# A second set of seven products in the first dense layer of a fused attention and MLP kernel

## The chip, the cores and the metric

The kernel runs on one core of one Trainium2 chip. The metric is the device time of one execution in microseconds (us); several executions are made and their median is given. Engines are called TensorE (PE, with PEld for its weight loads), VectorE (DVE), ScalarE (ACT), GpSimd (POOL) and SyncE (SP, which here issues DMAs). PSUM is the memory that TensorE writes; it has eight banks, and a tile of 128 x 512 f32 fills one.

## The reference: what is computed

Linear attention with decay over 4 batches, 8 heads, 768 positions and head size 64, then a two-layer MLP on the 3072 x 512 result:

```python
for b in range(nb):                                   # blocks of positions
    intra = einsum(qb, kb) * Dmask ; intra = intra @ vb
    inter = (qb * lam_pow) @ kv_state
    out[:, :, sl] = intra + inter
    kv_state = lam_block * kv_state + (kb * rev_pow).T @ vb
x = out as (3072, 512)
h = x @ w_in                                          # 512 -> 2048
g = h * tanh(softplus(h))                             # Mish
return g @ w_out                                      # 2048 -> 512
```

## The kernel before

**Groups.** The 768 positions are cut into six groups of 128 (`n` = 0 to 5). A group takes the same 128 positions of all four batches, so it has 512 tokens. For each group the kernel computes attention into `xt[n]` (512 features on 4 x 128 partitions, 512 tokens), the first layer and Mish into `hsg[n]` (16 units `ni` of 128 hidden features), and the second layer into the output. Attention of group n+1 is worked in between the matmuls of group n. There is no scheduler: the Python order of the calls is the order in every engine's queue. The loop from line 776 writes this order out: `units` is a list of short pieces of TensorE work, and after unit `u` come the extras that `visit`, `turns`, `sums`, `slots` and the last lines of the loop (L845) name for that number. "uN" below is unit N of that list.

**First layer.** `mm1_duo(n, g, lo, hi)` (L422) does units 2g and 2g+1 for half of the tokens: 8 matmuls of 128 x 256 into one `ph` bank, then one Mish on ScalarE (L441). In groups 2 to 5 (called `d` = 2 in the code) duos 0 to 5 cover units 0 to 11. Units 12 to 15 go through `set_unit` (L506): a Strassen-like product of 2 x 2 quarters (two input halves, two pairs of units, two token halves) with seven products P1 to P7 of 4 matmuls each, where a plain product takes 8 times 4. It needs sums of weight quarters (`isum`, made once in group 0), sums of quarters of `xt` (`xsum`, four VectorE operations, recorded at L496, after u6), and sums between products. Sums run through PSUM: P1's result is copied to SBUF (`u1`) and P2 added on top in the same bank; step "open" copies `u1` into another bank `z`, and P6 is added there; P6's sum is copied to a bank `y`, and P7 and P3 are added to `z` and `y`; P5's result is copied to SBUF (`p5`, ScalarE) and VectorE adds it to `z` and `y` (`hs`, L543) ahead of Mish; at the end P4 is added to `z`.

**Second layer.** `fast_unit` (L663) does the whole second layer by the same scheme in 14 units (seven products, two 128-token blocks each, 8 matmuls per unit). Its sums of `hsg` are `gsum` (`token_sum`, L574, VectorE).

**Attention in between.** `pair_a` (8 matmuls `pv`, then VectorE sums and the next state), `pair_s` (16 score matmuls `pS` and 16 state matmuls into the two `pO` banks, then four masked copies `sb` on VectorE) and `pair_o` (16 matmuls into the `pO` banks; four scalings `xtok` on VectorE at L384, and for each batch a transposing DMA from SP into `xt[n+1]`). Each handles two batches, and a group calls them for batches 0, 1 (s) and 2, 3 (t); t of group n fills the second token half of `xt[n+1]`. `turn` scales a k chunk (VectorE, `ktil`) and issues two transposing DMAs on SP (`qraw`, `kraw`).

**PSUM banks.** Tags and banks: `ph` 2, `po` 2, `pS`, `pk`, `pO`, `pq` one each. A matmul into a bank waits until the last reader of the bank's former tile is done.

**Loads.** k, q and v chunks are loaded by GpSimd's queue into `kn`, `qn` (8 buffers each) and `vz`, paced by one-element copies (`pace`) that wait for a Mish.

Of the kernel before, what the change touches and what calls it, by code (L numbers as in the profile page):

```python
# [7 lines left out]
F32 = mybir.dt.float32  # L8
# [12 lines left out]
def kernel(  # L21
# [125 lines left out]
    lbm = const.tile([128, JP, 128], F32, name="lbm")  # L147
# [22 lines left out]
    lq = const.tile([128, JP, C], F32, name="lq")  # L170
# [197 lines left out]
    def pair_o(s):  # L368

        n = s.n  # L370
        if xt[n] is None:
            xt[n] = work.tile([128, JP, GT], F16, name="xt", tag="xt", bufs=2)
        for t in range(2):
            for m, b in enumerate(s.bs):
                for j in range(JP):
                    nc.tensor.matmul(  # L376
                        s.pO[t][:, m, j, :], s.sb[m][t][:, j, :],
                        vz[(n * B + b) % NVB][:, 2 * j + t, 0:D],
                        start=False, stop=True, skip_group_check=True)
        xtok = [work.tile([128, JP, 2, D], F16, name="xtok", tag="xtok", bufs=4) for _ in s.bs]  # L380
        lt = lqt.rearrange("p (j t) -> p j t", t=2)
        for m, b in enumerate(s.bs):
            for t in range(2):
                nc.vector.tensor_tensor(out=xtok[m][:, :, t, :], in0=s.pO[t][:, m],  # L384
                                        in1=bc(lt[:, :, t], 2, D), op=ALU.mult)
            nc.sync.dma_start_transpose(
                out=xt[n][:, :, b * C : (b + 1) * C],
                in_=xtok[m].rearrange("p j t e -> p (j t e)"))
# [32 lines left out]

    def mm1_duo(n, g, lo, hi):  # L422

        if hsg[n] is None:
            hsg[n] = work.tile([128, NKI, GT], F16, name="hsg", tag="hsg", bufs=2)
        h = GT // 2
        half = lo // h
        if (n, g, half) not in duo_t:
            duo_t[n, g, half] = ps.tile([128, 2, h], F32, name="ph", tag="ph", bufs=2)
        t = duo_t[n, g, half]  # L430
        for m in range(2):
            ni = 2 * g + m
            for kc in range(NKC):
                nc.tensor.matmul(  # L434
                    t[:, m, lo - half * h : hi - half * h],
                    w_in(ni, kc),
                    xt[n][:, kc, lo:hi], start=(m == 0 and kc == 0), stop=(kc == NKC - 1),
                    skip_group_check=True,
                )
        if hi == half * h + h:  # L440
            nc.scalar.activation(hsg[n][:, 2 * g : 2 * g + 2, half * h : half * h + h], t, AF.Mish)  # L441
            mark.append(hsg[n][0:1, 2 * g, half * h : half * h + 1])
# [21 lines left out]
    SU = NKI - 4  # L464
    isum = [const.tile([128, KH, 256], F16, name=f"isum{i}") for i in range(4)]

    def i_quarter(r, c):

        t = win[-1]
        return t[:, r * KH : (r + 1) * KH, c * 256 : (c + 1) * 256]  # L470

    def in_sum(i):

        a, b, op = (
            lambda: (i_quarter(0, 1), i_quarter(0, 0), ALU.subtract),
            lambda: (i_quarter(1, 1), isum[0], ALU.subtract),
            lambda: (i_quarter(1, 1), i_quarter(0, 1), ALU.subtract),
            lambda: (i_quarter(1, 0), isum[1], ALU.subtract),
        )[i]()
        nc.vector.tensor_tensor(out=isum[i], in0=a, in1=b, op=op)  # L480
# [17 lines left out]
    first = {}  # L498

    def mish(n, r, c, src):  # L500

        nc.scalar.activation(
            hsg[n][:, SU + 2 * c : SU + 2 * c + 2, r * 2 * C : (r + 1) * 2 * C], src, AF.Mish)
        mark.append(hsg[n][0:1, SU + 2 * c, r * 2 * C : r * 2 * C + 1])

    def set_unit(n, step):  # L506
# [7 lines left out]
        def w_quarter_(r, c):  # L514
            return lambda kk, m: i_quarter(r, c)[:, kk, m * 128 : (m + 1) * 128]

        def w_part_(i):
            return lambda kk, m: isum[i][:, kk, m * 128 : (m + 1) * 128]

        key, lhs, rhs = {  # L520
# [7 lines left out]
            "open": lambda: (None,) * 3,  # L528
        }[step]()

        def place(key):
            if (n, key) not in first:
                tag, bufs = {"x": ("pS", 1), "z": ("po", 2), "w": ("po", 2), "y": ("pk", 1)}[key]
                first[n, key] = ps.tile([128, 2, 2 * C], F32, name=f"s{key}", tag=tag, bufs=bufs)
            return first[n, key]

        def kept(key, src, tag, bufs):
            first[n, key] = work.tile([128, 2, 2 * C], F32, name=key, tag=tag, bufs=bufs)
            nc.scalar.activation(first[n, key], src, AF.Copy)

        def plus_(r, key):
            o = work.tile([128, 2, 2 * C], F32, name="hs", tag="hs", bufs=2)
            nc.vector.tensor_tensor(out=o, in0=first[n, key], in1=first[n, "p5"], op=ALU.add)  # L543
            return lambda: mish(n, r, 1, o)

        if step == "open":
            place("w")
            nc.scalar.activation(place("z"), first[n, "u1"], AF.Copy)
            return
# [7 lines left out]
        if step == "P1":  # L557
            kept("u1", t, "osb", 4)
        elif step == "P2":
            mish(n, 0, 0, t)  # L560
        elif step == "P5":
            kept("p5", t, "p5", 1)
        elif step == "P6":
            nc.scalar.activation(place("y"), t, AF.Copy)
        elif step == "P7":
            plus_(1, "z")()
        elif step == "P3":
            plus_(0, "y")()
        elif step == "P4":
            mish(n, 1, 0, t)  # L570
# [65 lines left out]
    def after(n, step):  # L636
# [10 lines left out]
        elif step == "P5":  # L647
            p5[n] = work.tile([128, 2, HN], F32, name="p5", tag="p5", bufs=1)
# [92 lines left out]
    for u, (fn, args) in enumerate(units):  # L741
# [13 lines left out]
        if u == 8:  # L755
            for i in range(4):
                in_sum(i)
# [18 lines left out]
    for n in range(1, NG):  # L776
        r, s, t = Pair(), Pair(), Pair()
        r.n, r.bs, s.n, s.bs, t.n, t.bs = n, (2, 3), n + 1, (0, 1), n + 1, (2, 3)
        visit = {}
        d = 0 if n == 1 else 2  # L780
        if 1 < n < NG - 1:
            visit[3] = pair_a, r
        if n < NG - 1:
            visit[5 if d else 11] = pair_s, s
            visit[16 - d] = pair_o, s
            visit[26 - d] = pair_s, t
            visit[29 - d] = pair_o, t
        if n < NG - 2:
            visit[21 - d] = pair_a, s
        turns = {23 - d: (n + 2) * B, 25 - d: (n + 2) * B + 1}  # L790
        turns.update({3: (n + 1) * B + 2, 5: (n + 1) * B + 3} if d else {1: 9, 4: 10, 7: 11})

# [3 lines left out]
        def part(step):  # L796
            return set_unit, (n, step)

        if d:
            units = [[duo(g, 0)] for g in range(4)]  # L800
            units += [[part("P1"), duo(4, 0)], [part("P2"), duo(5, 0)]]
            units += [[duo(0, 1)], [duo(1, 1)], [part("open"), duo(2, 1)], [duo(3, 1)]]
            units += [[part("P5"), part("P6")], [duo(4, 1)], [part("P7"), part("P3")], [duo(5, 1), part("P4")]]
        else:
            units = [[duo(g, half)] for half in range(2) for g in range(NKI // 2)]
        steps = ("P1", "P5", "P6", "P2", "P7", "P3", "P4")
        units += [[(fast_unit, (n, step, blk))] for step in steps for blk in range(2)]
# [5 lines left out]
        if d:  # L813
            slots = range(4, 16)
            sums = {13: ((0, 0), (0, 1), (1, 0), (1, 1)), 17: ((2, 0),), 18: ((2, 1),), 20: ((3, 0),), 21: ((3, 1),)}
        else:
            slots = range(8, 16)
            sums = {9: ((2, 0),), 11: ((2, 1),), NKI - 3: ((0, 0), (1, 0)), NKI - 1: ((0, 1), (1, 1)),
                    NKI + 4: ((3, 0),), NKI + 5: ((3, 1),)}
        for u, calls in enumerate(units):  # L820
# [20 lines left out]
            if u in visit:  # L841
                f, s_ = visit[u]
                s_.spare = ("po", "po") if u < 12 else ("pS", "pk") if f is pair_a else ("ph", "po")
                f(s_)
            if d and u == 6:  # L845
# [32 lines left out]
```

## Time and profile before

| | us |
|---|---|
| median of 3 runs | 201.24 |
| the runs | 204.82, 200.41, 201.24 |
| the profiled execution | 200.12 |
| its span, first to last instruction | 198.4 |
| TensorE busy | 191.1 |
| VectorE busy | 142.6 |
| ScalarE busy | 98.3 |

Times of rows are counted from the start of the span. A row of the timeline or of the chain gives a start, a duration, an engine, a line and the operation; several instructions of one kind that follow each other are merged (x8). A recorded duration holds the engine's latency: the 128 x 256 matmul is recorded with 273 ns but the next one starts about 109 ns later, and VectorE and ScalarE operations overlap their neighbours by about 0.1 us as well. So the price of an operation in a full queue is the distance between starts, while someone who waits for its result waits for the whole duration.

### The profile page before, as it was taken

What the parts mean: (1) busy time and instruction counts of PE and PEld (TensorE: products, weight loads), DVE (VectorE), ACT (ScalarE), POOL (GpSimd) and SP (SyncE); (2) the same over time, 40 slices, a digit from 0 to 9 for tenths busy, and PEclk for the clock granted to TensorE, in tenths of its full rate; (3) what the DMA queues carried; (4) which work ended last, traced back from release to release, by engine and by line L of the source; (5) the groups of instructions that cost most, each with busy time, mean ns of one, the idle gap of its engine ahead of it and who ended that gap; (6) DMA issues with size and microseconds to landing.
All of it is one profiled execution on the core that took longest, in us unless ns stands there. A gap on an engine that the chain in (4) does not pass through costs nothing.

```text
span 198.4 us, 5083 instructions
## 1 busy us (share of the span) xinstructions
PE 191.1 (96%) x2065; PEld 159.0 (80%) x2065; DVE 142.6 (72%) x279; ACT 98.3 (50%) x174; POOL 79.7 (40%) x129
## 2 busy tenths in 40 slices
PE   7878999999999999999999999999999999999993
PEld 3654447878888998988998988998988988888882
DVE  7889289799944978685799685799695767322913
ACT  5694664423665421458520468530567530677320
POOL 7996333779487800038930038950044000000000
PEclk9999999999999999999999999999999999999999
DMA  8999999999999996759999759999759123600014
GB/s 127 141 156 198 207 206 202 154 172 187 191 143 181 156 135 165 185 109 114 128 129 168 183 108 132 137 106 209 191 88 149 8 56 106 159 3 0 3 55 159
DMA packets 112458, 26.82 MB, mean 135 GB/s; under 512 B 101554, under 2 KB 112434, under 8 KB 112434
## 3 DMA queue, kind: packets, MB, share of 16 engines
q0 software_dynamic: 77552, 13.37, 90.3%
q1 hardware_dynamic: 30848, 9.97, 26.8%
q10 hardware_dynamic: 4034, 3.15, 5.3%
q8 instruction: 16, 0.26, 0.6%
q14 instruction: 8, 0.07, 0.1%
HBM read 27.26 MB, written 6.29 MB: 169 GB/s over the span
## 4 chain that ended last, share of the span: by engine, by line
PE 92%; ACT 3%; DVE 3%; issue 1%; ACTq 0%
PE ph L434 28%; PE z L603 14%; PE x L603 11%; PE ph L405 7%; PE y L603 6%; PE w L603 5%; PE sz L553 3%; PE pS L349 2%; PE pO L376 2%; PE pO L255 2%; PE sx L553 2%; PE pv L328 1%; PE pS L234 1%; DVE dm L177 1%; PE pO L357 1%; ACT pkT L223 1%
## 5 line engine op out<-in xcount | busy, mean ns | idle before, releaser
L434 PE MATMUL ph<-xt,win 128*128 128x256 f16 x512 | 60.5, 273 | 0.0
L434 PEld LDWEIGHTS <-win 128*128 128x128 f16 x512 | 49.3, 98 | 6.0
L441 ACT ACTIVATE hsg<-ph 128x512 f16<-128x512 f32 x64 | 38.1, 595 | 20.0 <-PE ph L434 19.4
L603 PEld LDWEIGHTS <-gsum 128*128 128x128 f16 x384 | 36.8, 98 | 5.1 <-DVE gsum L589 0.3
L396 POOL COPY paced<-hsg 1x1 f16<-1x1 f16 x42 | 10.6, 252 | 52.1 <-ACT hsg L441 52.1
L603 PEld LDWEIGHTS <-hsg 128*128 128x128 f16 x272 | 26.1, 98 | 3.2
L589 DVE TENSOR_TENSOR gsum<-hsg 128x1024 f16<-128x1024 f16 x24 | 15.8, 688 | 11.6 <-ACT hsg L441 7.8
L603 PE MATMUL x<-wout,hsg 128*128 128x256 f16 x192 | 23.7, 273 | 0.0
L78 POOL DMA_DIRECT2D vz<-in_v_dram x24 | 21.1, 881 | 5.7 <-DMA wout<-in_moe_w_out_dram 1.7
L603 PE MATMUL z<-tsum,gsum 128*128 128x256 f16 x192 | 23.3, 273 | 0.0
L67 POOL DMA_DIRECT2D kn<-in_k_dram x23 | 20.5, 891 | 6.6 <-DMA win<-in_moe_w_in_dram 2.4
L75 POOL DMA_DIRECT2D qn<-in_q_dram x23 | 20.4, 888 | 5.7 <-DMA wout<-in_moe_w_out_dram 3.3
L365 DVE TENSOR_TENSOR sb<-pS,maskT 128x512 f16<-128x512 f32 x32 | 19.9, 683 | 1.7 <-PE pS L349 1.6
L265 DVE TENSOR_TENSOR ktil<-kn,lk 128x512 f16<-128x512 f16 (+1 forms) x22 | 14.9, 684 | 2.2 <-DMA kn<-in_k_dram 2.2
L288 DVE TENSOR_TENSOR raw<-pv,state 64x256 f32<-64x256 f32 x24 | 10.1, 422 | 7.4 <-PE pv L328 6.9
L660 ACT ACTIVATE osum<-z 128x512 f32<-128x512 f32 x5 | 3.0, 597 | 23.7 <-PE z L603 23.7
L405 PE MATMUL ph<-xt,win 128*128 128x512 f16 x64 | 14.5, 379 | 0.3 <-ACT xt L257 0.3
L417 ACT ACTIVATE hsg<-ph 128x512 f16<-128x512 f32 x16 | 9.6, 597 | 5.8 <-PE ph L405 5.8
L603 PE MATMUL y<-wout,gsum 128*128 128x256 f16 x96 | 12.3, 273 | 0.0
L405 PEld LDWEIGHTS <-win 128*128 128x128 f16 x64 | 6.1, 98 | 7.3 <-issue 0.5
L543 DVE TENSOR_TENSOR hs<-sz,p 128x512 f32<-128x512 f32 x4 | 2.8, 692 | 12.7 <-PE sz L553 10.5
L603 PE MATMUL w<-tsum,gsum 128*128 128x256 f16 x96 | 11.6, 273 | 0.0
(112 smaller groups left out, 266.7 us busy)
## 6 DMA issues: line engine op xcount, KB each, us to landing
vz<-in_v_dram POOLq DMA_DIRECT2D x24, 128.0 KB, 4.8
out_dram<-osum SPq DMA_DIRECT2D x12, 256.0 KB, 2.5
kn<-in_k_dram POOLq DMA_DIRECT2D x23, 128.0 KB, 5.7
qn<-in_q_dram POOLq DMA_DIRECT2D x23, 128.0 KB, 6.0
out_dram<-osum ACTq DMA_DIRECT2D x11, 256.0 KB, 2.8
wout<-in_moe_w_out_dram POOLq DMA_DIRECT2D x4, 512.0 KB, 16.5
win<-in_moe_w_in_dram POOLq DMA_DIRECT2D x3, 512.0 KB, 10.2
win<-in_moe_w_in_dram POOLq DMA_DIRECT2D x2, 256.0 KB, 5.8
```

Source lines behind the costliest of these rows:

```text
L67: nc.gpsimd.dma_start(out=kn[i], in_=chunk_rows(k, i))
L75: nc.gpsimd.dma_start(out=qn[i], in_=chunk_rows(q, i))
L78: nc.gpsimd.dma_start(out=vz[i % NVB][:, :, 0:D], in_=chunk_rows(v, i))
L265: (nc.gpsimd if B + 1 < i < 2 * B else nc.vector).tensor_tensor(out=t, in0=kn[i], in1=bc(lk, 2, D), op=ALU.mult)
L288: nc.vector.tensor_tensor(out=raw[rs, b % 2, j0 : j0 + nj, :], in0=pv[rs, :, rs], in1=olds(rs), op=ALU.add)
L365: nc.vector.tensor_tensor(out=s.sb[m][t], in0=sc[m][t], in1=bc(maskT, 1, JP), op=ALU.mult)
L396: nc.gpsimd.tensor_copy(paced, mark[-1])
L405: nc.tensor.matmul(ph_t[ni][:, lo:hi], w_in(ni, kc), xt[n][:, kc, lo:hi], start=(kc == 0), stop=(kc == NKC - 1),)
L434: nc.tensor.matmul(t[:, m, lo - half * h : hi - half * h], w_in(ni, kc), xt[n][:, kc, lo:hi], start=(m == 0 and kc == 0), stop=(kc == NKC ...
L441: nc.scalar.activation(hsg[n][:, 2 * g : 2 * g + 2, half * h : half * h + h], t, AF.Mish)
L589: nc.vector.tensor_tensor(out=gsum[n, i][:, ks, :], in0=a, in1=b, op=op)
L603: nc.tensor.matmul(places(n, key)[:, blk, lo:hi], lhs(kk, blk), rhs(kk, lo, hi), start=(fresh and kk == 0 and blk == 0), stop=(kk == HK - ...
```

## The change

Groups 2 to 5 only, apart from preparations in group 0. Units 8 to 11 also go through seven products: `set_unit` takes a set number `g` (0 for units 8 to 11, 1 for units 12 to 15), and each set has its own weight sums (made after u5 and u8 of group 0). Only duos 0 to 3 are left. The steps of both sets are done in turn, and the list is laid out anew:

| unit | before | after |
|---|---|---|
| u0 to u3 | duos 0 to 3, first half | P1 of both sets and duo 0; P2 of both and duo 1; duos 2, 3 (first half) |
| u4 to u6 | P1, duo 4; P2, duo 5; duo 0 (second half) | duo 0; "open" of set 1 and duo 1; "open" of set 0 and duo 2 (second half) |
| u7 to u9 | duo 1; "open", duo 2; duo 3 | P5, P6 of set 0; P5, P6 of set 1; duo 3 |
| u10 to u13 (after: to u12) | P5, P6; duo 4; P7, P3; duo 5, P4 | P7 of both; P3 of both; P4 of both, then two late Mish |
| second layer | u14 to u27 | u13 to u26 |
| `pair_a` of batches 2, 3; `pair_s` s; `pair_o` s | after u3; u5; u14 | after u0; u3; u13 |
| `pair_a` s; `pair_s` t; `pair_o` t | after u19; u24; u27 | after u17; u22; u25 |
| `turn`, four times | u3, u5, u21, u23 | u1, u2, u20, u23 |
| `x_sum` | after u6 | after u4 |

Other parts: P5's copy to `p5` moves from ScalarE to VectorE; P3's sum with `p5` is written back into its PSUM bank and its Mish reads it there, last of all ("late"); the scaling of `pair_o` s becomes 16 small ScalarE operations (four calls after u15, u16, u17, u19) where it was four VectorE operations; `pair_o` t stays on VectorE. The `kn` buffers go from 8 to 6, the `qn` buffers from 8 to 5, and `lbm` and `lq` share buffers with other tiles.

```diff
-        kn[i] = loads.tile([128, H, D], F16, name="kn", tag="kn")
+        kn[i] = loads.tile([128, H, D], F16, name="kn", tag="kn", bufs=6)
...
-        qn[i] = loads.tile([128, H, D], F16, name="qn", tag="qn")
+        qn[i] = loads.tile([128, H, D], F16, name="qn", tag="qn", bufs=5)
...
+        def scaled(m, t):
+            if put_off is None:
                 nc.vector.tensor_tensor(out=xtok[m][:, :, t, :], in0=s.pO[t][:, m],
                                         in1=bc(lt[:, :, t], 2, D), op=ALU.mult)
+            else:
+                for j in range(JP):
+                    nc.scalar.activation(xtok[m][:, j, t, :], s.pO[t][:, m, j, :], AF.Copy, scale=lt[:, j, t : t + 1])
...
+    homes = ({"x": ("pS", 1), "z": ("pS", 1), "w": ("po", 2), "y": ("pk", 1)},
+             {"x": ("pk", 1), "z": ("po", 2), "w": ("ph", 2), "y": ("ph", 2)})
...
+        if step == "hold":
+            place("w")
+            return
+        if step == "open":
+            nc.scalar.activation(place("z"), first[n, g, "u1"], AF.Copy)
+            return
+        if step == "late":
+            mish(0, 1, first[n, g, "y"])
+            return
...
         if step == "P1":
-            kept("u1", t, "osb", 4)
+            nc.scalar.activation(kept("u1"), t, AF.Copy)
...
         elif step == "P5":
-            kept("p5", t, "p5", 1)
+            nc.vector.tensor_copy(kept("p5"), t)
...
         elif step == "P7":
-            plus_(1, "z")()
+            o = work.tile([128, 2, 2 * C], F32, name="hs", tag="hs", bufs=2)
+            plus_p5("z", o)
+            mish(1, 1, o)
         elif step == "P3":
-            plus_(0, "y")()
+            plus_p5("y", t)
...
+            units = [part(0, "P1") + part(1, "P1") + [duo(0, 0)], part(0, "P2") + part(1, "P2") + [duo(1, 0)],
+                     [duo(2, 0)], [duo(3, 0)],
+                     [duo(0, 1)], part(0, "hold") + part(1, "open") + [duo(1, 1)], part(0, "open") + [duo(2, 1)],
+                     part(0, "P5", "P6"), part(1, "P5") + [(duo_bank, (n, 3, 1))] + part(1, "P6"), [duo(3, 1)],
+                     part(0, "P7") + part(1, "P7"), part(0, "P3") + part(1, "P3"),
+                     part(0, "P4") + part(1, "P4") + part(0, "late") + part(1, "late")]
...
+            sums = {8: ((2, 0),), 12: ((0, 0), (0, 1), (1, 0), (1, 1)), 14: ((2, 1),), 18: ((3, 0),), 19: ((3, 1),)}
...
+            if n > 1 and scales and u in (15, 16, 17, 19):
+                scales.pop(0)()
```

More of the change, by code (lines that the diff above doesn't have):

```diff
@@ L366, in pair_s, with pair_o @@
                     out=s.sb[m][t], in0=sc[m][t], in1=bc(maskT, 1, JP), op=ALU.mult)
-    def pair_o(s):
+    def pair_o(s, put_off=None):
         n = s.n
@@ L498, with set_unit, place, kept @@
     first = {}
[L500 to L506, printed above, removed]
+    homes = ({"x": ("pS", 1), "z": ("pS", 1), "w": ("po", 2), "y": ("pk", 1)},
+             {"x": ("pk", 1), "z": ("po", 2), "w": ("ph", 2), "y": ("ph", 2)})
+    def set_unit(n, g, step):
+        def place(key):
+            if (n, g, key) not in first:
+                tag, bufs = homes[g][key]
+                first[n, g, key] = ps.tile([128, 2, 2 * C], F32, name=f"s{key}{g}", tag=tag, bufs=bufs)
+            return first[n, g, key]
+        def kept(key):
+            first[n, g, key] = work.tile([128, 2, 2 * C], F32, name=key, tag=key, bufs=2)
+            return first[n, g, key]
+        def mish(r, c, src):
+            ni = NKI // 2 + 4 * g + 2 * c
+            dst = hsg[n][:, ni : ni + 2, r * 2 * C : (r + 1) * 2 * C]
+            nc.scalar.activation(dst, src, AF.Mish)
+            mark.append(dst[0:1, 0, 0:1])
+        def plus_p5(key, out):
+            nc.vector.tensor_tensor(out=out, in0=first[n, g, key], in1=first[n, g, "p5"], op=ALU.add)
         def x_quarter(r, c):
@@ L527, in set_unit @@
             "P4": lambda: ("z", w_part_(3), x_quarter(1, 1)),
-            "open": lambda: (None,) * 3,
         }[step]()
[L531 to L549, printed above, removed]
         t = place(key)
@@ L778, with part @@
         r.n, r.bs, s.n, s.bs, t.n, t.bs = n, (2, 3), n + 1, (0, 1), n + 1, (2, 3)
[L779 to L791, printed above, removed]
         def duo(g, half):
             return mm1_duo, (n, g, half * (GT // 2), (half + 1) * (GT // 2))
[L796 to L807, printed above, removed]
+        def part(g, *steps):
+            return [(set_unit, (n, g, step)) for step in steps]
         later = []
@@ L812 @@
             later += [lambda f=f, i=(n + 2) * B + b: f(i) for b in range(B) for f in (load_k, load_q)]
-        if d:
-            slots = range(4, 16)
[L815 to L819, printed above, removed]
+        if n == 1:
+            units = [[duo(g, half)] for half in range(2) for g in range(NKI // 2)]
+            visit = {11: (pair_s, s), 16: (pair_o, s), 21: (pair_a, s), 26: (pair_s, t), 29: (pair_o, t)}
+            turns = {1: 9, 4: 10, 7: 11, 23: 12, 25: 13}
+            slots = range(8, 16)
+            sums = {9: ((2, 0),), 11: ((2, 1),), 13: ((0, 0), (1, 0)), 15: ((0, 1), (1, 1)), 20: ((3, 0),), 21: ((3, 1),)}
+        else:
+            units = [part(0, "P1") + part(1, "P1") + [duo(0, 0)], part(0, "P2") + part(1, "P2") + [duo(1, 0)],
[4 more added lines that the diff above has]
+                     part(0, "P4") + part(1, "P4") + part(0, "late") + part(1, "late")]
+            visit = {}
+            if n < NG - 1:
+                visit = {0: (pair_a, r), 3: (pair_s, s), 13: (pair_o, s), 22: (pair_s, t), 25: (pair_o, t)}
+            if n < NG - 2:
+                visit[17] = pair_a, s
+            turns = {1: (n + 1) * B + 2, 2: (n + 1) * B + 3, 20: (n + 2) * B, 23: (n + 2) * B + 1}
+            slots = range(4, 16)
+            sums = {8: ((2, 0),), 12: ((0, 0), (0, 1), (1, 0), (1, 1)), 14: ((2, 1),), 18: ((3, 0),), 19: ((3, 1),)}
+        steps = ("P1", "P5", "P6", "P2", "P7", "P3", "P4")
+        units += [[(fast_unit, (n, step, blk))] for step in steps for blk in range(2)]
+        scales = []
         for u, calls in enumerate(units):
@@ L842 @@
                 f, s_ = visit[u]
-                s_.spare = ("po", "po") if u < 12 else ("pS", "pk") if f is pair_a else ("ph", "po")
-                f(s_)
-            if d and u == 6:
+                s_.spare = ("po", "po") if u < 13 else ("pS", "pk") if f is pair_a else ("ph", "po")
+                if f is pair_o and s_ is s and n > 1:
+                    f(s_, scales)
+                else:
+                    f(s_)
+            if n > 1 and scales and u in (15, 16, 17, 19):
+                scales.pop(0)()
+            if n > 1 and u == 4:
                 for i in range(4):
```

67 lines of the change are left out of this document (38 added, 29 removed).

## The prediction

> **What bounds the kernel now.** I read the page first, then the waits of TensorE, then the chain of work in order of time, then the timeline of one group.
>
> ```profile
> span 198.4 us, 5083 instructions
> ...
> PE 191.1 (96%) x2065; PEld 159.0 (80%) x2065; DVE 142.6 (72%) x279; ACT 98.3 (50%) x174; POOL 79.7 (40%) x129
> ...
> PE   7878999999999999999999999999999999999993
> ...
> PE 92%; ACT 3%; DVE 3%; issue 1%; ACTq 0%
> ```
>
> TensorE is busy in every slice from the fifth on, and the chain that ends last is TensorE for 92%. A busy row could still hide waits, so the waits of its matmuls come next: six kinds, of which these are the first and the last.
>
> ```profile
> PE busy L157 <- DVE kzero L141: 1.2, 1, 1.2
> ...
> PE ph L405 <- ACT xt L257: 0.3, 1, 0.3
> ```
>
> None lies in the groups that the change touches. There the chain is one matmul after another; this is most of the first layer of group 3.
>
> ```profile
> 113.97 0.45 PE pv L328 x8
> 114.42 0.44 PE sx L553 x4
> 114.85 0.87 PE ph L434 x8
> ...
> 117.03 0.55 PE pS L349 x16
> 117.59 0.23 PE pO L357 x16
> 117.82 3.60 PE ph L434 x32
> 121.42 0.44 PE sw L553 x4
> ```
>
> So the prices on TensorE: a duo 0.87 (0.109 for each matmul), a product 0.44, `pair_a` 0.45, `pair_s` 0.78. With no gaps, each matmul taken away saves its 0.109, and each new wait costs its whole length. The other engines have room, but VectorE's is small in the second layer (second row; columns PE, PEld, DVE, ACT):
>
> ```profile
> 110.44:125.43 14.99, 14.99 (x167) 13.22 (x165) 10.15 (x22) 10.13 (x19) 7.68 (x16) 1.00 1.16 147
> 125.43:139.93 14.50, 14.50 (x186) 12.99 (x185) 13.46 (x26) 4.07 (x8) 5.65 (x9) 1.00 1.55 150
> ```
>
> **What is removed.** Set 0 takes 28 matmuls where duos 4 and 5 took 32: 4 fewer in each of four groups, 16 x 0.109 = 1.75 us. That is 0.9%, and the most that the change can give. Group 1 keeps its list. Everything below asks which new waits eat the 1.75.
>
> **Clocks of hand-over.** From the timeline:
>
> ```profile
> 113.81 0.61 PE L328 MATMUL pv<-vz,ktil 128*128 128x128 f16 x8
> ...
> 116.62 0.68 DVE L265 TENSOR_TENSOR ktil<-kn,lk 128x512 f16<-128x512 f16 x1
> ...
> 116.97 0.62 PE L349 MATMUL pS<-qraw,kraw 64*128 64x128 f16 x16
> ...
> 117.62 2.48 DVE L365 TENSOR_TENSOR sb<-pS,maskT 128x512 f16<-128x512 f32 x4 [0.32 <-PE pS L349]
> ...
> 120.02 0.42 DVE L496 TENSOR_TENSOR xsum<-xt 128x512 f16<-128x512 f16 x1
> ...
> 120.47 0.42 DVE L496 TENSOR_TENSOR xsum<-xsum,xt 128x512 f16<-128x512 f16 x1
> ...
> 121.26 0.60 PE L553 MATMUL sw<-xsum,isum 128*128 128x256 f16 x4
> ...
> 123.08 0.60 PE L553 MATMUL sz<-xsum,isum 128*128 128x256 f16 x4
> ...
> 123.79 0.69 DVE L543 TENSOR_TENSOR hs<-sz,p 128x512 f32<-128x512 f32 x1 [2.22 <-PE sz L553]
> ```
>
> A product begun at 123.08 lets VectorE start at 123.79: 0.71 later. In the other direction:
>
> ```profile
> 8.23 0.59 ACT L223 ACTIVATE pqT<-pq 128x512 f16<-128x512 f16 x1
> ...
> 8.87 0.40 PE L234 MATMUL pS<-pqT,pkT 64*128 64x128 f16 x8 [0.30 <-ACT pqT L223]
> ```
>
> The copy ends at 8.82 and the matmul starts 0.05 later.
>
> **Step 1, `xsum` behind `pair_s` (groups 2 to 4).** Let s be the start of `pair_s`. VectorE does the four `sb`, then `xsum`: the first starts at s + 3.05 and ends at s + 3.47, and P5 may start at s + 3.52. Before, four duos stood between and P5 started at s + 4.29, with room. After, three do: 0.78 + 3 x 0.87 = s + 3.40. Wait 0.12. The two `turn` ahead do not add to it: `pair_a` now starts 1.75 into the group (two products each of 0.44 and a duo), the first `ktil` 2.81 later as in the rows, the second ends 1.28 after that, at 5.84; `pair_s` starts at 5.69 and `sb` 0.65 later, at 6.34. This wait is a difference of sums that hold to about 0.1, so its bounds are 0 and 0.22.
>
> **Step 2, duo 3 behind P5's copy (groups 2 to 5).** In the built program the first matmul of duo 3, second half, waits for VectorE: it gets the `ph` bank that P5 of set 1 wrote, and must wait until `tensor_copy` has brought that to `p5`. If that P5 starts at p, the copy starts at p + 0.71; duo 3 is due after P5 and P6, at p + 0.87. The trace has no copy of f32 out of PSUM on VectorE; the nearest rows:
>
> ```profile
> L365 DVE TENSOR_TENSOR sb<-pS,maskT 128x512 f16<-128x512 f32 x32 | 19.9, 683 | 1.7 <-PE pS L349 1.6
> ...
> L221 DVE COPY pqT<-pq 128x512 f16<-128x512 f16 x2 | 0.8, 420 | 0.4 <-PE pq L211 0.4
> ...
> L697 DVE CAST q<-qn 128x512 f16<-128x512 f32 x1 | 0.4, 427 | 0.0
> ```
>
> If it takes 0.42, duo 3 starts at p + 1.18 (wait 0.31), if 0.68, at p + 1.44 (wait 0.57). I take 0.68: `sb` has the same source, f32 in PSUM, while CAST reads SBUF and COPY reads f16. Below 0.31 the wait cannot fall unless the copy beats every 512-wide row. The first `p5` copy and the last two `xsum` fill VectorE until just then, which costs no more. Four times 0.57 = 2.28. [...]
>
> **Step 3, ScalarE at P6 and P2.**
>
> ```profile
> 109.81 0.63 PE L376 MATMUL pO<-vz,sb 128*128 128x64 f16 x16
> 110.01 0.60 ACT L660 ACTIVATE osum<-z 128x512 f32<-128x512 f32 x1 [5.54 <-PE z L603]
> ...
> 110.64 0.38 ACTq L625 DMA_DIRECT2D out_dram<-osum  x1
> ...
> 119.71 0.60 ACT L441 ACTIVATE hsg<-ph 128x512 f16<-128x512 f32 x1 [0.28 <-PE ph L434]
> 120.20 0.60 ACT L548 ACTIVATE sz<-u 128x512 f32<-128x512 f32 x1
> ```
>
> In a queue ScalarE starts an operation every 0.49. After u4 ends (e), it has Mish (e + 0.24), "open" of set 1, Mish, "open" of set 0 (e + 1.71, done e + 2.31): P6 of set 0 may start at e + 2.36. It is due at e + 2.18, in groups 2 to 4 at 2.30 because of step 1: waits 0.18 once and 0.06 three times. At a group's start ScalarE is held by the last output copy and its DMA issue until 1.2 after the last P4 (109.81 to 111.02). The two `u1` copies then end at 1.81 and 2.30. In groups 2 to 4 P2 of set 0 is due at 2.20 and does not wait. Group 5 has no `pair_a`: due at 1.75, it starts at 1.86, and P2 of set 1, due 0.44 later, waits another 0.05: 0.16 together. Nothing excludes 0 for any of these; twice the sizes is the upper bound.
>
> **Edits that I cost at nothing, and their cover.** The new weight sums after u5 of group 0, four of 0.42, fall into an idle time of VectorE:
>
> ```profile
> 25.22 0.69 DVE L589 TENSOR_TENSOR gsum<-hsg 128x1024 f16<-128x1024 f16 x1 [2.76 <-ACT hsg L417]
> ```
>
> They need 1.7 of its 2.76; if their weights came too late for that, up to 1.7 would be lost once. The smaller `kn` and `qn` make GpSimd's loads wait only for chunks that were read a whole group earlier, and nobody is behind them that TensorE needs soon. VectorE gains two copies and two sums and loses four scalings in a group. The thinnest cover is that of the `hs` sums: if P7 of set 0 starts at a, they start at a + 0.71 and a + 1.31, the second lets P4 of set 1 start at a + 2.04, and that is due after five products, at a + 2.18; what is late there is paid in full. `gsum` for the fast P5 is done about 0.7 ahead, since `pair_o` stands in between. The P3 sum in place and the late Mish are read only by `gsum` of P3, ten units on. If a cover of this kind is gone, each tenth costs 0.3 to 0.4 over the groups.
>
> **Sum.** Groups 2 to 4: 3 x (0.12 + 0.57 + 0.06) = 2.25. Group 5: 0.57 + 0.18 + 0.16 = 0.91. Together 3.16, less 1.75: +1.41. The profiled execution took 200.12 (198.4 span and 1.7 around it), so 201.5. The median of the three runs is 1.1 above that execution, the fastest 0.3.
>
> **Rivals.**
>
> *First: the waits are short.* If the copy takes 0.42, the four waits shrink by 0.26 each and the sum is +0.37, 200.5. If duo 3 does not wait at all it is -0.87, 199.2; with none of the waits, 198.4. For it: all waits are differences of long sums, good to about 0.1. Against: the copy would have to beat `sb`.
>
> *Second: the scaling on ScalarE is late.* The 16 small operations stand ahead of the fast layer's `y` copy, which P7 waits for. At a distance d between them the copy lets P7 start late by 12 d - 3.83: from the end of P1, 0.24 + 0.49 for the `z` copy, four d, 0.49 for the `p5` copy, eight d, 0.65 for the `y` copy and the hand-over, against six units and `pair_a` on TensorE, 5.70.
>
> ```profile
> L195 ACT ACTIVATE lqt<-lnb,eq 128x8 f32<-128x8 f32 x1 | 0.3, 284 | 0.0
> L692 ACT ACTIVATE lbh<-lnb 128x8 f32<-128x8 f32 x1 | 0.2, 208 | 0.0
> ```
>
> A scale from memory costs 0.076 here, and 64 columns some 0.05 more: 0.33 long, and d at most that, at least 0.22 with the overlap of long rows. At 0.33 P7 is 0.13 late three times, 201.9. Over 2% it decides from d = 0.39 on. [...]
>
> *Third, on the slower side: `xt` lands late.* u4 needs `xt` of the second half, now 6.5 after the group's start where it was 7.5. Ahead of it on SP stand the second `turn`, whose `ktil` is now behind the `sb`, and two stores.
>
> ```profile
> 140.22 0.54 SPq L625 DMA_DIRECT2D out_dram<-osum  x1
> 140.85 3.39 SPq L386 DMA_TRANSPOSE xt<-xtok  x2
> ...
> xt<-xtok SPq DMA_TRANSPOSE x16, 2.7
> ```
>
> From the end of the transposes of s, 4.9 before the group's start, SP has four transposes of `turn` at 1.25, two stores at 0.55 and the first `xt`: the second is issued at 2.4 and lands at 5.1. A delay beyond 1.4 is paid in three groups; 2% slower needs 0.86 more in each, a delay of 2.2. That is two or three issues as long as the slow one here (3.39 for two). Then 204.1 and more. For it: slow issues do occur, and the `ktil` wait is new on SP. Against: nothing waited for `xt` before with 1.5 to 2 us to spare.
>
> **How the numbers follow.** Forecast 0.5, its own range 200.6 to 202.5; first rival 0.27 (198.4 to 200.5); second 0.08 (201.9 and up); third 0.15, of which 0.1 over 2%. Two per cent, about what a measurement of this kernel can tell from no change, is 4 us: faster would be below 197.2, under the 198.4 without any wait, 0.03 for what I overlook; slower 0.15; same 0.82. The range drops the lowest tenth of the first rival and the worst of the third: 198.8 to 203.9.
>
> **What would show it.** TensorE's waits should list duo 3's `ph` behind VectorE four times, near 0.57; `sw` behind `xsum` three times, near 0.12; `sz` behind ScalarE, under 0.2. A `p5` copy near 0.42 proves the first rival's half, a wait of `z` on `y` the second, of `ph` on `xt` the third. I am wrong if duo 3 does not wait, or if a group loses over 1.3 us.

## The result, and the profile after

The changed kernel takes 201.49 us (median of 17 runs), the kernel before 200.74 beside it: ratio 1.005 (95%: 1.0033 to 1.0068). The ratios here and below leave out single slow runs (such as 204.82 before and 204.54 after) and are estimates with an interval, so they can differ by 0.001 to 0.002 from the quotient of the two medians. The change saves sixteen matmuls and is a little slower, well inside the 2% that the prediction allowed for "same". The prediction was 201.5.

The profiled execution of the changed kernel took 202.27 us. From its page:

```profile
span 200.5 us, 5119 instructions
...
PE 190.2 (95%) x2049; PEld 157.4 (79%) x2049; DVE 149.6 (75%) x287; ACT 111.3 (55%) x230; POOL 78.8 (39%) x129
```

TensorE issues 2049 matmuls where it issued 2065, as meant, and is busy 0.9 us less, yet the span is 2.1 longer. So the loss is in waits. TensorE's waits (total, times, longest) name two that the kernel before did not have in groups 2 to 5 (`p` and the last `xt`), and one at the start, behind `vz`:

```profile
PE pO L255 <- DMA vz<-in_v_dram: 1.7, 1, 1.7
PE ph L453 <- DVE p L583: 1.4, 4, 0.4
PE busy L157 <- DVE kzero L141: 1.2, 1, 1.2
...
PE ph L453 <- DMA xt<-xtok: 0.2, 1, 0.2
```

The second is the wait that step 2 foretold: duo 3 of the second half, behind the `p5` copy of set 1, once in each of groups 2 to 5. This is the place in group 2, TensorE first:

```profile
92.39 0.60 PE L574 MATMUL sw<-xsum,isum 128*128 128x256 f16 x4
92.83 0.60 PE L574 MATMUL sz<-xsum,isum 128*128 128x256 f16 x4
93.80 0.92 PE L453 MATMUL ph<-xt,win 128*128 128x256 f16 x7 [0.37 <-DVE p L583]
```

```profile
92.13 0.42 DVE L514 TENSOR_TENSOR xsum<-xt,xsum 128x512 f16<-128x512 f16 x1
92.46 1.28 DVE L583 COPY p<-sw 128x512 f32<-128x512 f32 x2
```

P5 of set 1 begins at 92.39, the second of the two copies ends at 93.74, duo 3 starts at 93.80. After P6 (92.83 + 4 x 0.109 = 93.27) it was due: 0.53 is lost. The wait in brackets is 0.37, because the row of a matmul ends about 0.16 after its successor could have started. The same difference hides every stall shorter than 0.16 from the list of waits; they show only in the distances between starts. The four losses are 0.53, 0.51, 0.53 and 0.51.

The wait of 1.7 us is for a load at the very start, ahead of anything that the change touches. To compare the two kernels I therefore use new profiles of both (experiments e9 and e10), from the first product of group 0 to the first `fin` product of the last group. The kernel before:

```profile
16.81 1.04 PE L405 MATMUL ph<-xt,win 128*128 128x512 f16 x4 [0.28 <-DMA win<-in_moe_w_in_dram]
...
95.78 1.04 PE L603 MATMUL x<-wout,hsg 128*128 128x256 f16 x8
...
125.27 0.93 PE L603 MATMUL x<-wout,hsg 128*128 128x256 f16 x7
...
193.13 1.93 PE L678 MATMUL fin<-tsum,hsg 128*128 128x256 f16 x24
```

The changed kernel:

```profile
16.78 1.02 PE L418 MATMUL ph<-xt,win 128*128 128x512 f16 x4 [0.25 <-ACT xt L257]
...
96.19 1.04 PE L626 MATMUL x<-wout,hsg 128*128 128x256 f16 x8
...
125.82 0.93 PE L626 MATMUL x<-wout,hsg 128*128 128x256 f16 x7
...
193.94 1.26 PE L701 MATMUL fin<-tsum,hsg 128*128 128x256 f16 x12
```

That stretch, called the body below, is 176.32 before and 177.16 after. Of the 0.84, 0.28 is lost once in group 0, where a second-layer product starts late behind a weight sum that VectorE had to hold back for the last load of w_out. VectorE, then TensorE:

```profile
36.18 0.69 DVE L480 TENSOR_TENSOR tsum<-wout,tsum 128x1024 f16<-128x1024 f16 x1 [0.74 <-DMA wout<-in_moe_w_out_dram]
```

```profile
35.78 1.04 PE L626 MATMUL x<-wout,hsg 128*128 128x256 f16 x8
36.93 1.03 PE L626 MATMUL z<-tsum,gsum 128*128 128x256 f16 x8
```

What is left, 0.56, lies in groups 2 to 5 and is the change's own. Whether the 0.28 belongs to the change as well is open. All five profiles of kernels built from the changed one in which the first product starts by 16.9 (e1, e4, e6, e8, e10) lose 0.2 to 0.45 at this place; the two of the kernel before with such a start lose nothing. A group from `x` to `x` takes 29.49 before and 29.63 after.

### The profile page after: what moved, and what is told of

Its sections match the earlier page's. It is cut to its first block, busy times and chain, and to the rows that moved or that the text cites. A ratio compares the mean times of both kernels' runs of the same rounds, so it can differ in the third digit from the quotient of the medians.

```text
span 200.5 us, 5119 instructions
## 1 busy us (share of the span) xinstructions
PE 190.2 (95%) x2049; PEld 157.4 (79%) x2049; DVE 149.6 (75%) x287; ACT 111.3 (55%) x230; POOL 78.8 (39%) x129
## 4 chain that ended last, share of the span: by engine, by line
PE 80%; DVE 8%; DMA 5%; POOL 4%; issue 1%; ACT 0%; DVEq 0%; POOLq 0%
PE ph L453 17%; PE z L626 14%; PE x L626 10%; PE ph L418 7%; PE y L626 5%; PE w L626 5%; PE sz L574 4%; DMA vz<-in_v_dram 4%; PE sx L574 3%; PE pS L349 2%; DVE sb L365 2%; DVE p L583 2%; PE pO L376 2%; PE sy L574 2%; DVE xsum L514 1%; POOL kn L67 1%
## 5 line engine op out<-in xcount | busy, mean ns | idle before, releaser
L453 PE MATMUL ph<-xt,win 128*128 128x256 f16 x384 | 45.0, 273 | 1.6 <-DVE p L583 1.4
L453 PEld LDWEIGHTS <-win 128*128 128x128 f16 x384 | 37.1, 98 | 6.8 <-issue 2.4
L460 ACT ACTIVATE hsg<-ph 128x512 f16<-128x512 f32 x48 | 28.7, 597 | 15.6 <-PE ph L453 15.3
L409 POOL COPY paced<-hsg 1x1 f16<-1x1 f16 x42 | 9.8, 233 | 56.4 <-ACT hsg L460 55.9
L574 PEld LDWEIGHTS <-isum 128*128 128x128 f16 x128 | 12.4, 97 | 2.3 <-issue 0.3
L430 ACT ACTIVATE hsg<-ph 128x512 f16<-128x512 f32 x16 | 9.6, 597 | 5.8 <-PE ph L418 5.8
L653 DVE TENSOR_TENSOR osum<-z,p 128x512 f32<-128x512 f32 x6 | 4.1, 689 | 10.8 <-issue 6.0
L626 PE MATMUL y<-wout,gsum 128*128 128x256 f16 x96 | 11.8, 273 | 0.0
L418 PEld LDWEIGHTS <-win 128*128 128x128 f16 x64 | 6.1, 97 | 7.3 <-issue 0.5
```

The lines of the kernel that those rows point to most:

```text
L418: nc.tensor.matmul(ph_t[ni][:, lo:hi], w_in(ni, kc), xt[n][:, kc, lo:hi], start=(kc == 0), stop=(kc == NKC - 1),)
L453: nc.tensor.matmul(t[:, m, lo - half * h : hi - half * h], w_in(ni, kc), xt[n][:, kc, lo:hi], start=(m == 0 and kc == 0), stop=(kc == NKC ...
L574: nc.tensor.matmul(t[:, m, :], lhs(kk, m), rhs(kk), start=(step in ("P1", "P5") and m == 0 and kk == 0), stop=(kk == KH - 1), skip_group_c ...
L626: nc.tensor.matmul(places(n, key)[:, blk, lo:hi], lhs(kk, blk), rhs(kk, lo, hi), start=(fresh and kk == 0 and blk == 0), stop=(kk == HK - ...
```

## The experiments

**e1_swap: the bank taken away from the wait.** The waits indicate that a tile gets its `ph` bank at its first use, and not where the program asks for it: `duo_bank` asks for duo 3's tile ahead of P6, yet duo 3 waits for P5's copy. In the change the copy of P6 into `y` uses its tile ahead of duo 3, so `y` gets the bank that Mish of duo 2 frees, and duo 3 gets P5's. Here the copy comes after duo 3's matmuls, ahead of its Mish:

```diff
+        if between:
+            between()
         if hi == half * h + h:
...
+        if step == "hand":
+            nc.scalar.activation(place("y"), first[n, g, "z"], AF.Copy)
+            return
...
-        elif step == "P6":
+        elif step == "P6" and g == 0:
             nc.scalar.activation(place("y"), t, AF.Copy)
...
-                     part(0, "P5", "P6"), part(1, "P5") + [(duo_bank, (n, 3, 1))] + part(1, "P6"), [duo(3, 1)],
+                     part(0, "P5", "P6"), part(1, "P5", "P6"),
+                     [(mm1_duo, duo(3, 1)[1] + (lambda n=n: set_unit(n, 1, "hand"),))],
```

> Duo 3 of the second half gets the ph bank that Mish of duo 2 has freed, and the sum y of set 1 gets the bank of P5: the copy of P6 of set 1 into y is issued after the matmuls of duo 3 and ahead of its Mish. Theory (the wait of duo 3 for the p5 copy is on the path and paid in full): the four waits of 0.53, 0.50, 0.52 and 0.50 us go, nothing takes their place (the y copy waits for the p5 copy instead, ends about 2.04 us after P5 begins, and P7 of set 1 is due at 2.18), so 201.49 - 2.05 = 199.4 us, ratio to the kernel before 0.993 (0.991 to 0.996). Rival (the stall moves: P7 of set 1 now waits for y, or P4 of set 1 for the hs sum): at least half of it stays, 200.5 us or more, ratio 0.999 or more, with the new wait named in TensorE's waits. Rival (the lost gain is at the start, where the profiled run had a wait of 1.7 us for vz): the ratio falls by 0.010 all the same, but first products of group 0 start near 18.1 us in the profile again; near 16.8 us would make that wait chance.

Measured: 198.88 us, ratio 0.990 (0.9875 to 0.9916). Here are the same place of group 2 on TensorE and ScalarE's `y` copy:

```profile
91.44 0.60 PE L579 MATMUL sw<-xsum,isum 128*128 128x256 f16 x4
91.88 0.60 PE L579 MATMUL sz<-xsum,isum 128*128 128x256 f16 x4
92.32 1.04 PE L453 MATMUL ph<-xt,win 128*128 128x256 f16 x8
93.19 1.04 PE L579 MATMUL sz<-xsum,isum 128*128 128x256 f16 x8
```

```profile
92.89 0.58 ACT L562 ACTIVATE sy<-sz 128x512 f32<-128x512 f32 x1 [0.62 <-DVE p L588]
```

Duo 3 follows P6 without a gap. Now ScalarE waits for the `p5` copy, which costs nothing: `y` is there at 93.47, and P7 of set 1 is due at 93.63. The body is 175.11, of which 0.31 is the late load of w_out again: 174.80, against 176.88 for the changed kernel without its 0.28. The difference, 2.08, is the sum of the four waits. The theory is confirmed in the trace. The ratio lies just below the expected 0.991 to 0.996: the medians differ by 2.61, and the further 0.5 has no counterpart in the groups. Of the rivals, the moved stall falls; the other, a slower start, falls too, since the first product begins at 16.89 here.

**e2_best and e8_best_again: the small waits as well.** On top of e1_swap:

```diff
                     out=s.sb[m][t], in0=sc[m][t], in1=bc(maskT, 1, JP), op=ALU.mult)
+                if between and (m, t) == (0, 0):
+                    between()
...
-                     [duo(0, 1)], part(0, "hold") + part(1, "open") + [duo(1, 1)], part(0, "open") + [duo(2, 1)],
...
+                     [duo(0, 1)], part(0, "hold") + part(0, "open") + [duo(1, 1)], part(1, "open") + [duo(2, 1)],
...
+                if f is pair_s and u == 3:
+                    f(s_, lambda: [x_sum(n, i) for i in range(2)])
...
-                for i in range(4):
+                for i in range(0 if n == NG - 1 else 2, 4):
```

> As e1_swap, and the first two xsum go between the third and the fourth sb of pair_s, and the copies open change places (set 0 first). Theory: besides the 2.05 us of duo 3, the two waits of P5 for xsum (0.11 and 0.10 us) and the four waits of P6 for open (0.05, 0.16, 0.06, 0.16 us) go, together 0.64: 201.49 - 2.69 = 198.8 us, ratio 0.990 (0.988 to 0.993). Rival (these small waits are differences that move elsewhere): no better than e1_swap, ratio within 0.001 of it.

> The kernel of e2_best once more, since its profile has groups 2 to 5 shorter by 0.4 us than e1_swap (29.01 for 29.10 in groups 2 to 4, 27.35 for 27.52 in group 5), while its median was not lower and its first layer of group 0 began 0.65 us later behind a wait of 1.2 us for a load of w_in. Theory (the loads at the start make each run's time wander by up to 1 us, and the small waits are paid): median 198.3 to 198.8 us, ratio 0.987 to 0.990, and the groups again 29.0. Rival (what the small waits give is lost elsewhere): 199.0 us or more, with groups of 29.1.

Measured: 199.02 us, ratio 0.990 (0.9875 to 0.9927), and 198.81, 0.991 (0.9889 to 0.9927). The first profile has a body of 174.40, the second 174.96 with two waits for loads in it (0.34 and 0.22), so 174.40: 0.41 less than e1_swap. The waits of P5 and P6 are gone (0.64), and a new one of 0.08 stands in groups 2 to 4 (P3, 0.23 together). The groups are 29.01 long, as e8 expected. The times, though, do not tell the two kernels apart: what the start adds varies more from run to run than 0.41. So neither statement wins outright: the times are no better than those of e1_swap, as the rival of e2 has it, while in the trace the small waits are gone and 0.41 of them is gained.

**e3_twice: the suspected cost doubled.**

```diff
             nc.vector.tensor_copy(kept("p5"), t)
+            if g == 1:
+                nc.vector.tensor_copy(first[n, g, "p5"], t)
```

> The changed kernel with the p5 copy of set 1 made twice, the same data into the same place, so that the bank comes free one VectorE operation (0.58 to 0.6 us from start to start) later. Theory: duo 3 waits so much longer in each of four groups, 4 x 0.59 = 2.4 us: 203.9 us, ratio to the kernel before 1.016, and the recorded waits of duo 3 go from about 0.35 to about 0.95. Rival (TensorE gets the time back later, since other stalls behind it shrink): under 1.2 us more, ratio under 1.011.

Measured: 204.28 us, ratio 1.017 (1.0145 to 1.0192). In group 3:

```profile
122.00 1.28 DVE L583 COPY p<-sw 128x512 f32<-128x512 f32 x2
123.32 0.69 DVE L585 COPY p<-sw 128x512 f32<-128x512 f32 x1
```

```profile
124.06 1.05 PE L453 MATMUL ph<-xt,win 128*128 128x256 f16 x8 [1.10 <-DVE p L585]
```

The four losses are 1.24 to 1.26, about 0.73 more each, and the body is 179.91, 3.0 above the changed kernel's 176.88: the wait is paid in full. The extra copy cost 0.72, not 0.59: the copy before it started at 122.60 (0.60 after its neighbour), and this one only 0.72 later, at 123.32. It writes where the former writes, and it starts 0.04 after the former's end at 123.28, so here the two do not overlap.

**e4_vecscale: scaling back on VectorE.**

```diff
-                if f is pair_o and s_ is s and n > 1:
+                if f is pair_o and s_ is s and n > NG:
                     f(s_, scales)
```

> The changed kernel with the scaling of pair_o s back on VectorE (four operations in place of 16 small ones on ScalarE). Theory (the scaling on ScalarE is hidden, since the 16 operations pass at 0.22 us each and the y copy is in time): 201.5 us, ratio within 0.003 of the changed kernel's 1.005. It can only lose, if VectorE now brings gsum late: three groups by up to 0.6 us. Rival (the ScalarE queue costs TensorE time in the second layer): 0.4 us or more faster, ratio 1.003 or less.

Measured: 201.18 us, ratio 1.0018 (1.0001 to 1.0035). The groups take 29.63, 29.62, 29.63 and 28.02, the changed kernel's (e10) 29.62, 29.63, 29.62 and 28.02. By its ratio alone this is the rival's case (1.003 or less, 0.3 us less than the changed kernel). The groups decide against it: the 0.3 us has no counterpart in them, so the scaling is hidden on either engine, as the theory has it.

**e5_hs: the thin cover of the `hs` sums.** On top of e1_swap the first `hs` sum is made twice:

```diff
             plus_p5("z", o)
+            if g == 0:
+                plus_p5("z", o)
```

> The kernel of e1_swap with the first hs sum (set 0) made twice, the same data into the same place: one VectorE operation of 0.60 us from start to start ahead of the second hs sum. It asks whether the cover of the hs sums is as thin as costed (0.13 us to spare ahead of P4 of set 1; the changed kernel's rows give about 0.15). Theory: P4 of set 1 waits 0.60 - 0.15 = 0.45 us in each of four groups, 1.8 us: 198.9 + 1.8 = 200.7 us, ratio to the kernel before 0.999. Rival (the spare time is larger, or P4 does not wait for the sum): below 199.6 us, ratio under 0.994.

Measured: 201.80 us, ratio 1.004 (1.002 to 1.0062). VectorE and TensorE in group 3:

```profile
124.11 2.02 DVE L541 TENSOR_TENSOR hs<-sz,p 128x512 f32<-128x512 f32 x3 [0.49 <-ACT sy L562]
```

```profile
125.58 1.19 PE L579 MATMUL sz<-xt,isum 128*128 128x256 f16 x8 [0.25 <-DVE hs L541]
126.61 1.04 PE L633 MATMUL x<-wout,hsg 128*128 128x256 f16 x8
```

Three sums take 2.02, so the repeated one costs 0.73 (a pair takes 1.29). P4 of set 0 starts at 125.58, 0.42 late, and that of set 1 another 0.16 (the row takes 1.19 where others of its kind take 1.04): 0.58 per group, which is 0.73 less the 0.13 to 0.15 that were to spare. The body is 177.12, 2.32 above e1_swap's 174.80. The cover was as thin as costed; the expectation missed by the price of a repeated operation, and the median by a further 0.6 that the groups don't show.

**e6_p5_scalar: the `p5` copies back on ScalarE.**

```diff
-            nc.vector.tensor_copy(kept("p5"), t)
+            nc.scalar.activation(kept("p5"), t, AF.Copy)
```

> The changed kernel with the p5 copies of both sets back on ScalarE. Theory (duo 3 waits for whichever engine copies P5 of set 1): ScalarE has the Mish of duo 2 and the y copy of set 0 ahead, starts the copy of set 1 about 0.87 us after that P5 begins and ends it at 1.47, so duo 3 waits about 0.65 us where it waited 0.51: 0.4 to 0.6 us more over four groups, 202.0 us, ratio 1.007. Rival (the wait was VectorE's load, the xsum and sb ahead of the copy): duo 3 waits less than 0.3 us, 200.7 us or less, ratio 1.000 or less.

Measured: 202.44 us, ratio 1.010 (1.0063 to 1.0137). Group 3 on ScalarE and TensorE:

```profile
121.72 0.62 ACT L585 ACTIVATE sy<-sz 128x512 f32<-128x512 f32 x1
122.24 0.62 ACT L583 ACTIVATE p<-sw 128x512 f32<-128x512 f32 x1
```

```profile
121.34 0.60 PE L574 MATMUL sw<-xsum,isum 128*128 128x256 f16 x4
...
122.91 1.03 PE L453 MATMUL ph<-xt,win 128*128 128x256 f16 x8 [0.53 <-ACT p L583]
```

The copy starts 0.90 after P5, behind the `y` copy of set 0, and duo 3 loses 0.69 to 0.70, 0.18 more than with VectorE. The wait follows the bank, not VectorE's load: the rival falls.

**e7_xt_late: the third rival's delay made on purpose.** The last `turn` of groups 2 and 3 issues its two transposing DMAs twice:

```diff
                 turn(turns[u])
+                if n in (2, 3) and u == 23:
+                    for to, src in ((qraw, qn), (kraw, ktil)):
+                        nc.sync.dma_start_transpose(out=to[turns[u]], in_=src[turns[u]].rearrange("p h c -> p (h c)"))
```

> The changed kernel with the last turn of groups 2 and 3 issuing its two transposing DMAs twice (same data, same place): SP is busy 2.5 us longer ahead of the transposes of xt for the second half of groups 3 and 4. It measures the spare time of xt, which the third rival of the prediction put at 1.4 us; in the profiled run of the changed kernel one issue of 2.47 us in place of 1.23 made u4 of group 3 wait 0.23, so about 1.0. Theory: u4 waits 1.1 to 1.8 us in each of the two groups, 2.9 us together: 204.4 us, ratio 1.018 (1.012 to 1.023). Rival (SP or the transposes have more room than the rows show): under 1 us, ratio under 1.010.

Measured: 210.12 us, ratio 1.046 (1.0432 to 1.0489), 8.6 us more than the changed kernel where 2.9 were expected. SP ahead of group 3's second half, and u4:

```profile
113.18 1.19 SPq L860 DMA_TRANSPOSE qraw<-qn  x1
114.46 1.22 SPq L860 DMA_TRANSPOSE kraw<-ktil  x1
115.77 0.53 SPq L648 DMA_DIRECT2D out_dram<-osum  x1
116.39 2.54 SPq L392 DMA_TRANSPOSE xt<-xtok  x2
```

```profile
120.29 4.45 PE L453 MATMUL ph<-xt,win 128*128 128x256 f16 x24 [2.72 <-DMA xt<-xtok]
```

The last `xt` is issued by 118.93 and used at 120.29, 1.36 later; u4 was due at 117.51, so 2.78 is lost (2.59 in group 4). The repeated pair held SP longer than 2.5 us, since it waited for the first pair to land (SP's waits: total, times, longest):

```profile
SPq L860 <- DMA qraw<-qn: 1.3, 2, 1.1
```

The store is issued at 115.77 where the row before the pair, ended at 112.04, would have allowed 112.1. That is 3.6 us later, and so the spare time of `xt` was about 0.9 here; in group 4 the delay was 4.1 and the spare time 1.5. The two agree once the first pair of group 3 is looked at: one of its issues (`kraw` at 110.20) took 1.84 us where 1.22 is usual, and without that 0.62 the spare time is 1.5 here too.

But the two waits are only 5.4 of the 8.6. The row of u4 to u6 says where the rest is: 24 matmuls take 4.45, and 2.79 elsewhere. By stretches (columns: PE, PEld, DVE, ACT, POOL, then the granted clock):

```profile
117.00:120.00 3.00, 0.57 (x26) 0.45 (x24) 2.48 (x4) 0.35 (x1) 0.00 (x0) 1.00 0.66 157
120.00:121.00 1.00, 0.71 (x6) 0.65 (x7) 0.71 (x2) 0.00 (x0) 0.00 (x0) 0.90 0.66 131
121.00:122.00 1.00, 1.00 (x7) 0.67 (x6) 0.80 (x3) 0.25 (x1) 0.00 (x0) 0.50 0.46 90
122.00:123.00 1.00, 1.00 (x6) 0.67 (x5) 0.00 (x0) 0.84 (x2) 0.18 (x1) 0.50 0.31 61
123.00:124.00 1.00, 1.00 (x6) 0.73 (x5) 0.00 (x0) 0.54 (x2) 0.72 (x1) 0.50 0.63 128
124.00:125.00 1.00, 1.00 (x10) 0.83 (x9) 0.00 (x0) 0.77 (x3) 0.63 (x3) 0.90 0.85 126
```

After the idle 2.7 us the clock granted to TensorE reads 0.50 for about 3.4 us (a row of 0.90 holds 0.2 us at half), from 0.5 us after the work resumed (0.9 in group 4). If the 1.66 by which 4.45 exceeds 2.79 falls within these 3.4 us, a matmul then starts an estimated 0.213 after the one before, not 0.109. That cost another 1.67, and 1.65 in group 4: 2.78 + 2.59 + 1.67 + 1.65 = 8.7. The groups themselves are 8.4 longer, since the short waits of P5 and P6 (steps 1 and 3 of the prediction) vanish behind these delays. The 0.50 followed idle stretches of 2.72 and 2.52 us here, while the clock stayed at 1.00 after those of 1.71 (`vz`) and 1.10 (e3_twice). Whether the length alone decides is not shown.

**e9 to e11: the start, and the buffers.** e9 and e10 are the two kernels unchanged; e11 is the kernel before with `bufs=6` for `kn` and `bufs=5` for `qn`.

> The kernel before, unchanged, for a second look at its start. Theory (the loads of the first 37 us land at times that wander, so the wait of 1.7 us for vz in the profile of the changed kernel was chance): the body, from the first product of group 0 to the end, is 181.6 us again within 0.4, and the first product starts anywhere from 16.6 to 18.2 us. Rival (the kernel before always has its last part of w_out by 35.7 us and its first product at 16.8): both come again within 0.1.

> The changed kernel, unchanged, for a second look. Theory: the four waits of duo 3 come again at 0.50 to 0.53 us, the wait of 1.7 us for vz and that of 0.23 us for xt in group 3 do not both come again, and groups 2 to 5 take 29.62, 29.62, 29.62 and 28.02 us; ratio to the kernel before 1.003 to 1.007. Rival (the start is slower by the change): first product again at 18.0 us or later, behind vz.

> The kernel before with the smaller kn and qn buffers of the changed one (6 and 5 in place of 8), and nothing else of the change. Theory (these buffers are free long before they are loaded again, so the edit costs nothing): 200.8 us, ratio 1.000 (0.998 to 1.002). Rival (the loads of later chunks are held back and the last part of w_out or the loads of the next groups come late): 0.4 us or more slower, ratio 1.002 or more, with the last part of w_out after 36.1 us in the profile, as in the kernels built from the changed one.

Measured: e9 200.15 us, one run, body 176.32 (176.30 in the first profile). e10 202.06, ratio 1.0055 (1.0022 to 1.0089). e11 200.85, ratio 1.0014 (0.9993 to 1.0035), body 176.32. So no cost of the buffers is seen, and more than 0.35% is excluded. One sign of e11's rival is there all the same: the sum that waits for the last part of w_out starts at 36.24 in e11 (35.69 and 35.92 in the two profiles of the kernel before), but the first product began late as well, at 17.50, so that nothing was lost. A loss of the size seen in the five profiles above (0.2 to 0.45), paid only after an early start, therefore stays possible. In e10 duo 3 loses 0.53, 0.53, 0.53 and 0.51 again, `xt` is not waited for, and the product that had waited 1.7 us for `vz` starts 1.36 earlier. From the first profile, then from e10:

```profile
16.85 0.62 PE L255 MATMUL pO<-sb,vz 128*128 128x128 f16 x8 [1.71 <-DMA vz<-in_v_dram]
```

```profile
15.49 0.61 PE L255 MATMUL pO<-sb,vz 128*128 128x128 f16 x8
```

So that wait does not come with the change, and none of the other profiles has it at that length; which load is late differs (`vz`, `win`, `qn`, the last part of `wout`). One thing stays open: the runs of the changed kernel spread wider (200.5 to 203.0 in e10) than those of the kernel before beside them (200.2 to 202.1, all but two below 201.0), and no profile of it caught a run above 202.3.

## Why the prediction came out as it did

**Removed, 1.75.** Right: 16 matmuls at 0.109. The groups of e8 are 0.48 shorter than before (29.01 against 29.49), 0.44 of it the four matmuls.

**Step 2, 2.28.** Right in its mechanism and nearly in size: 2.08 in the first profile, 2.10 in e10; removing it gave 2.08, lengthening it was paid one for one. The choice between the two ends was the copy's price, in the first profile of the changed kernel:

```profile
L583 DVE COPY p<-sw 128x512 f32<-128x512 f32 x8 | 5.3, 685 | 3.5 <-PE sw L574 3.4
```

685 ns: the end taken from `sb` (683 ns before the change), and the first rival falls. The wait was about 0.05 shorter because the copy started 0.67 after P5 in groups 2 to 4 and 0.64 in group 5, not 0.71.

**Step 1, 0.36.** 0.11 in each of the three groups of e10, near the 0.12 worked out. **Step 3, 0.36 and 0.16.** 0.06 three times and 0.16 at P6; 0.16 and 0.05 at P2 of group 5. Together that is 0.55, where 0.52 was predicted.

**What the sum missed.** The prediction read the list of waits as saying that none lies in these groups of the kernel before, so that only new waits count. There were some, too short for that list. One of 0.08 stood in each of groups 2 to 5, ahead of P7. In group 2 duo 4 begins at 92.65 and is 0.87 long, so P7 was due at 93.52:

```profile
92.65 1.04 PE L434 MATMUL ph<-xt,win 128*128 128x256 f16 x8
93.60 0.60 PE L553 MATMUL sz<-xsum,isum 128*128 128x256 f16 x4
```

Another of 0.16 stood in the last second layer, and 0.035 was lost early in each of groups 3 to 5. None of these is left in the changed kernel, which gains 0.59. With that, the sum is -1.75 - 0.59 + 2.10 + 0.32 + 0.34 + 0.21 = +0.63, and the body shows +0.56. The prediction had +1.41. That it met 201.5 is luck: it added this to an execution of 200.12, while the median before is 200.74, and the medians differ by 0.75. A base that is 0.62 too low and a difference that is 0.66 too large cancel. The mechanism of step 2 is not luck, as e1, e3 and e6 show. The traces account for 0.56 in the groups and, in e10, the 0.28 of w_out; what the start adds in the other runs is not known.

**Edits costed at nothing.** The buffers (e11), VectorE's load and the scaling (e4) show no cost in the groups; the late w_out load in group 0 is the open point. The `hs` sums had 0.13 to 0.15 to spare (e5).

**Second rival.** It needed a distance of 0.32 or more between the small scalings to make P7 late at all. Eight took 1.74 us:

```profile
131.77 1.74 ACT L389 ACTIVATE xtok<-pO,lqt 128x64 f16<-128x64 f32 x8
133.52 0.58 ACT L669 ACTIVATE y<-z 128x512 f32<-128x512 f32 x1
```

With 335 ns recorded for one, that is 0.20 from start to start, below the 0.22 that the prediction put as the least. `y` is done at 134.10 and P7 starts at 135.01, on time.

**Third rival.** Its mechanism is real: one slow issue on SP (2.47 us where 1.23 is usual) gave the 0.23 of group 3 in the first profile. Its spare time was put at 1.4; e7 shows 1.5, of which one slow issue in group 3 took 0.6. Its price was put too low: with losses of 2.6 and 2.8 us to the late `xt`, the stretches at a granted clock of 0.50 added 1.7 each time.

## What to carry to other kernels

When a change shares one bank among more tiles, find out which tile gets which bank, and whose last reader a matmul will then wait for: here the order of two first uses decided over 2 us, more than the saved matmuls brought, and exchanging them turned a loss of 0.5% into a gain of 1%. Read stalls from distances between starts: the list of waits left out those shorter than 0.16 us here, and they came to 0.59 in the kernel before. Add a forecast difference to the median of several runs rather than to one profiled execution.

## What the runs showed of the hardware

- After idle stretches of 2.52 and 2.72 us the granted clock of TensorE was 0.50 for about 3.4 us (e7); after 1.71 and 1.10 us it was 1.00 (first profile of the changed kernel, e3). Each of the two stretches at 0.50 cost another 1.7 us.
- Two VectorE operations on 128 x 512 f32 that write the same tile followed each other at 0.72 to 0.73 us, those of the same size that write different tiles at 0.60 (e3, e5).
- In e7 the repeated transposing DMA into the same tile waited for the first to land (1.3 us in two waits, the longest 1.1), and the issues behind it on SP waited as well (SP idle from 112.04 to 113.18).
